# Named PSUM bank pairs, the sine table at the first cosine, a third block transposed whole, and one rounding of each softmax batch on VectorE

## The chip, the core and the metric

The kernel runs on one core of a Trainium2 chip. Its metric is the device time of one execution in microseconds. Engines: PE (TensorE), PEld (its weight loads), DVE (VectorE), ACT (ScalarE), POOL (GpSimd), SP (SyncE, which issues all DMAs here). PSUM has eight banks; a tile of 128x1024 f32 takes two.

## The reference

Two stages, all float32. The first is a causal convolution over 7 rows whose weights are a softmax over 7 numbers given for each row and head; the second is a feed-forward network whose activation is `h * cos(h)`.

```python
# x (8,4096,192), weight_gen (8,4096,8,7): 8 heads of 24 columns, 7 taps
w = np.exp(weight_gen - max);  w = w / (sum(w) + 1e-9)
out = np.einsum('bshk,bskhg->bshg', w, x_unf)      # x_unf: the row and the 6 before it
x2 = out.reshape(32768, 192)
h = x2 @ w_in            # (192, 2048)
g = h * np.cos(h)
return g @ w_out         # (2048, 192)
```

## The kernel before, in words

The 32768 rows are 64 blocks of 512 rows (4 rows on each of 128 partitions). A block's 2048 hidden columns are 8 pairs of 128-column chunks. The main loop runs over all 512 pairs; one turn of it, `i`, is called a period here (block `i // 8`, pair `i % 8`). The order of the instructions on each engine is the order in which the code emits them; nothing is moved later.

In period `i` these things are emitted, in this order:

- ACT rounds `h` of pair i-1 plus 0.25 to an integer (`act_turns`, L365), and writes the rounded-to-fp32r copy of `h * cos` of pair i-2 (`act_hi`, L383). In one period of every 32 (step `EXP`) ACT also takes the exponential of the next softmax batch here (L205).
- DVE subtracts the integer from `h` (`dve_fraction`, L369); ACT takes the sine of that fraction (`act_cos`, L373); DVE writes the remainder of pair i-2 in bf16 (`dve_lo`, L387), the last reader of that `h`; DVE multiplies `h` by the cosine, in place in PSUM (`dve_g`, L376).
- In periods 1 to 8, pieces of the two weight matrices are converted as well (`two_parts`): an Abs on ACT into PSUM (L130), a shift (L132) and two bit operations (L136, L140) on DVE, casts on ACT (L143, L145) and a subtraction on POOL (L146) one period later. The PSUM scratch of the three DVE steps is a tile of the same pool as `h`, taken in `make_room`.
- PE multiplies: the first half of the products of `h` of pair i (`ffn_in_first`, L338), the sums over the hidden columns for pair i-6's quarter (`ffn_out`, L417), and the second half of `h` (`ffn_in_second`, L355). SP holds an empty instruction behind the first half, which the second half waits for (`traded`). ACT copies finished sums out of PSUM every second period (`evacuate`, L440 and L444); the next sums need the bank.
- POOL does two or three steps of the convolution of a later block (`attention`, L257 products and L272 additions, 13 instructions a block).

The pool `ps_h` has three pairs of banks under one name; a tile gets the pair that became free first when its first instruction comes up. In a period without conversions, `h` of pair i takes the pair of banks that pair i-3 left. `ps_m` holds the sums in the other two banks.

A block's convolution result is transposed by PE before it can be multiplied. Blocks 1 and 2 (`WHOLE = 2`) are transposed by eight 128x128 transposes in one go (`transpose_all`, L308) in pair 5 of the block before, into the banks that `h` takes next, and are copied out by ACT (L664); their remainder is made on DVE (L299). From block 3 on, the transposes are small 64x64 pieces (L317) between the sums of block b-2, sixteen for a block, and the remainder is made on POOL (L299). POOL's convolution of block 3 has to be emitted by period 14 for that.

Ahead of the loop a prologue converts the first pieces, does the convolution of block 0 (three rows on DVE, one on POOL) and takes the first exponentials. ACT keeps one set of function tables; a load (ACT_TABLE_LOAD) stands where the next function is in another set.

Of the kernel before, what the change touches and what calls it, by code (L numbers as in the profile page):

```python
# [20 lines left out]
P = 128  # L21
# [22 lines left out]
def tile_softmax_conv_then_cos_ffn(  # L44
# [25 lines left out]
    HALF = NPAIR // 2  # L70
    LAG = 6
    TR = 5
    WHOLE = 2
    TMP = 4
    CW = 512

# [2 lines left out]
    work = ctx.enter_context(tc.tile_pool(name="work", bufs=2))  # L79
    ps_h = ctx.enter_context(tc.tile_pool(name="ps_h", bufs=3, space=bass.MemoryType.PSUM))  # L80
    ps_m = ctx.enter_context(tc.tile_pool(name="ps_m", bufs=1, space=bass.MemoryType.PSUM))


    x_v = x.rearrange("n (q r) d -> q n (r d)", r=RPP)
# [27 lines left out]

    room = []

    def make_room():
        sizes = ps_h.tile([P, 2, CT], F32, name="h")
        bits = work.tile([P, 2, CW], F32, name="t1", tag="turn", bufs=TMP)
        room[:] = [(sizes[:, n, 0:CW].bitcast(I32), bits[:, n, :].bitcast(I32)) for n in range(2)]

# [179 lines left out]
        eng.tensor_tensor(  # L299
            out=lo[:, :, cs], in0=t, in1=hi[:, :, cs].bitcast(F32), op=ALU.subtract)  # L300

    def transpose_all(b, tr=None):
        xa = mixed[b]
        if tr is None:
            tr = ps_h.tile([P, 2, CT], F32, name="h")
        for part in range(2):
            for r in range(R):
                nc.tensor.transpose(tr[:, part, r * P:(r + 1) * P], xa[:, r, columns(part)], ident)  # L308
        transposed.add(b)
        return tr  # L310
# [18 lines left out]
    def ffn_in_first(i, h=None):  # L329

        b, pair = divmod(i, NPAIR)
        x_hi, x_lo = xT[b]
        if h is None:
            h = ps_h.tile([P, 2, CT], F32, name="h")
        for m, (w, v) in enumerate(((wa_hi, x_lo), (wa_lo, x_hi), (wa_hi, x_hi))):
            for q in range(2):
                rs = slice(q * D2, (q + 1) * D2)
                nc.tensor.matmul(  # L338
                    h[:, q, :], lhsT=w[rs, chunk(pair, q)], rhs=v[rs, q, :],
                    start=(m == 0), stop=False, skip_group_check=True)  # L340
        hs[i] = h
        traded(h)
# [19 lines left out]
    def act_turns(i):  # L362
        t = work.tile([P, 2, CT], F32, name="turn", bufs=TMP)
        turns[i] = t
        nc.scalar.activation(out=t.bitcast(I32), in_=hs[i], func=AF.Identity, bias=0.25, scale=1.0)  # L365

    def dve_fraction(i):
        t = turns[i]
# [101 lines left out]
    def last_half():  # L470

        b = NB - 1
        tiles = [ps_h.tile([P, 2, CT], F32, name="h") for _ in range(2)]
        for p in range(HALF):
            for lo in range(2):
                g = g_parts[b * NPAIR + HALF + p][lo]
                for t in range(R):
                    acc = tiles[t // 2][:, t % 2, 0:(D if lo else 2 * D)]
                    for n in range(2):
                        fc = 2 * (HALF + p) + n  # L480
                        nc.tensor.matmul(
                            acc, lhsT=g[:, n, t * P:(t + 1) * P], rhs=(wo_b if lo else wo)[:, fc, :],
                            start=(p == 0 and lo == 0 and n == 0),
                            stop=(p == HALF - 1 and lo == 1 and n == 1), skip_group_check=True)
        fin = work.tile([P, R, D], F32, name="fin")
        for t in range(R):
            old = sums.pop((b, t // 2))[:, t % 2] if t % 2 else sums[(b, t // 2)][:, 0]
            part_ = work.tile([P, 2, CT], F32, name="part1", bufs=2)
            part = part_[:, 0, 0:2 * D]
            nc.vector.tensor_tensor(out=part, in0=tiles[t // 2][:, t % 2, 0:2 * D], in1=old, op=ALU.add)  # L490
            (nc.vector if t == R - 1 else nc.gpsimd).tensor_tensor(
                out=fin[:, t, :], in0=part[:, 0:D], in1=part[:, D:2 * D], op=ALU.add)
            if t % 2:
                nc.sync.dma_start(out=o_v[:, :, (b * R + t - 1) * D:(b * R + t + 1) * D],
                                  in_=fin[:, t - 1:t + 1, :].rearrange("p r d -> p (r d)"))
# [19 lines left out]
    def all_of(*steps):  # L515
        steps = list(steps)
        while steps:
            steps = [s for s in steps if next(s, steps) is not steps]
# [11 lines left out]
    def load_weights(period):  # L530
        for when, at, load, args in late:
            if when == period:
                converts.setdefault(at, []).append(load(*args))
# [1 line left out]
    nc.scalar.activation(out=early, in_=early, func=AF.Exp)  # L535

    RV = 3
    own = ps_h.tile([P, 2, CT], F32, name="h")
    own = own.rearrange("p a b -> p (a b)")
    own_acc = own[:, 0:RV * D].rearrange("p (r d) -> p r d", d=D)  # L540
    own_taps = own[:, R * D:R * D + RV * H * K].rearrange("p (n k) -> p n k", k=K)
# [13 lines left out]
    def go_on(steps, n):  # L555
        for _ in range(n):
            next(steps, None)
# [11 lines left out]
    all_of(sm1)  # L569
    bg = attentions()  # L570
    go_on(bg, 1)
    make_room()
    go_on(w_a0, 1)
    go_on(w_b0, 1)
    all_of(mix_v)
    tr = transpose_all(0)
    go_on(w_a0, 3)
    go_on(w_b0, 3)
    first = split(0, tr, slice(0, CT), nc.vector)
# [1 line left out]
    all_of(w_a0, w_b0)  # L581
    all_of(first)
    go_on(sm2, 2)
    make_room()
    go_on(w_a1, 4)
    go_on(sm2, 1)
    nc.scalar.activation(out=early, in_=early, func=AF.Sin)
    all_of(w_a1)
    go_on(bg, 4)

    N = NB * NPAIR
# [4 lines left out]
    for i in range(N + LAG + 1):  # L596
# [11 lines left out]
        converts_now = converts.get(i, ())  # L608
        h_now = None
        if converts_now:  # L610
            h_now = ps_h.tile([P, 2, CT], F32, name="h")

        whole = None
        if pair == TR and b + 1 <= WHOLE:
            until_mixed(b + 1)
            whole = transpose_all(b + 1, h_now)
        if 0 <= j and j % (2 * R) == 0 and WHOLE < j // (2 * R) + 2 < NB:
            until_mixed(j // (2 * R) + 2)

        def products():  # L620
            if b < NB and pair == 0:
                assert b in transposed
            if whole is not None and j >= 0:

                ffn_out(j)
                ffn_in_first(i, whole)
            elif j >= N - HALF:
                if j == N - HALF:
                    last_half()
                return  # L630
            elif busy and EXP + 2 <= step <= EXP + 3:

                ffn_out(j, rest=False)
                ffn_in_first(i)
                ffn_out(j, rest=True)
            else:
                if i < N:
                    ffn_in_first(i, h_now if whole is None else whole)
                if j >= 0:
                    ffn_out(j)  # L640
            if i < N:
                ffn_in_second(i)
            if j in stores:
                stores.pop(j)()
            if j >= 0:
                evacuate(j)


        early_sums = busy and step == EXP + 1
        if 0 <= i - 1 < N:  # L650
            act_turns(i - 1)
        if early_sums:
            products()
# [15 lines left out]
        if 0 <= i - 2 < N:  # L669
            dve_lo(i - 2)  # L670
        if converts_now:
            make_room()
        for c in converts_now:
            next(c)
        all_of(*converts.pop(i - 1, ()))
        for c in now:
            next(c)
        splits.extend(later)
        if 0 <= i - 1 < N:
            dve_g(i - 1)  # L680
        for _ in range(3):
            for c in converts_now:
# [3 lines left out]
            break  # L686
        if not early_sums:
            products()
        load_weights(i)
        if step in SOFTMAX and step != EXP or NPAIR - 2 <= i < NPAIR + 1:  # L690
            next(sm, None)
        for _ in range(3 if i < 12 or i < 64 and i % 4 == 0 else 2):
            next(bg, None)


# [39 lines left out]
```

## Time and profile before

| | |
|---|---|
| median of 3 runs | 2276.68 us (2276.4 to 2276.85) |
| profiled execution | 2278.1 us, span 2276.3 us |
| busy | PE 2212.3 (97%), PEld 2017.7, DVE 1904.1 (84%), ACT 1896.8 (83%), POOL 2003.6 (88%) |
| granted TensorE clock | 0.992 of full speed over the span |

The page cuts the span into 40 slices of 57 us. PE is at 3 and 7 tenths in the first two and at 9 or more in all others:

```profile
PE   3799999999999999999999999999999999999998
DVE  7788888888888888888888888888888888888887
ACT  4688888888888888888888888888888888888886
POOL 7799989998999989989899899989989899899941
PEclk9799999999999999999999999999999999999999
```

A digit is the busy share in tenths, and in the line PEclk the granted clock in tenths of full speed.

### The profile page before, as it was taken

Reading aid. Unit: us, or ns where it says so; the run is one execution under the profiler, and the core shown is the slowest. Engines: PE = TensorE matmul, PEld = TensorE weight load, DVE = VectorE, ACT = ScalarE, POOL = GpSimd, SP = SyncE. Lnnn points to the kernel's source line nnn. Section 1 sums busy time; section 2 is a strip of 40 time slices with the busy share of each in tenths; the row PEclk is TensorE's granted clock in tenths of the full one; section 3 lists DMA queues with packets and bytes.
Section 4 is the critical chain, followed back from the end, with each engine's and each line's share of the span. In section 5 each row is a group of like instructions: output and inputs, shape, how many; then the busy total and the mean of one; then the engine's idle time right before and its main releaser. Section 6 shows DMA issues by size and latency. Waiting matters only on the chain.

```text
span 2276.3 us, 60636 instructions
## 1 busy us (share of the span) xinstructions
PE 2212.3 (97%) x26504; PEld 2017.7 (89%) x26504; DVE 1904.1 (84%) x1647; ACT 1896.8 (83%) x2129; POOL 2003.6 (88%) x1464
## 2 busy tenths in 40 slices
PE   3799999999999999999999999999999999999998
PEld 2688888889898898998999999998998989999887
DVE  7788888888888888888888888888888888888887
ACT  4688888888888888888888888888888888888886
POOL 7799989998999989989899899989989899899941
PEclk9799999999999999999999999999999999999999
DMA  6211221211211211211211212212212212212100
GB/s 155 56 44 41 50 51 33 58 43 33 58 41 43 50 40 44 50 47 37 58 30 46 58 28 56 50 28 57 50 34 50 58 26 50 58 26 52 33 9 22
DMA packets 25767, 105.55 MB, mean 46 GB/s; under 512 B 2734, under 2 KB 6566, under 8 KB 25502
## 3 DMA queue, kind: packets, MB, share of 16 engines
q1 hardware_dynamic: 25502, 101.67, 18.2%
q8 instruction: 208, 3.41, 0.6%
q14 instruction: 57, 0.47, 0.1%
HBM read 76.50 MB, written 25.17 MB: 45 GB/s over the span
## 4 chain that ended last, share of the span: by engine, by line
PE 68%; POOL 19%; ACT 7%; issue 3%; DVE 3%; DMA 0%; POOLq 0%; SPq 0%; ACTq 0%; DVEq 0%
PE acc L417 32%; PE h L355 23%; PE h L338 12%; POOL xa L272 6%; POOL pr L257 5%; POOL part L456 2%; ACT turn L365 2%; ACT part L440 2%; POOL x_lo L299 1%; ACT ghi L383 1%; POOL fin L457 1%; DVE turn L369 1%; ACT turn L373 1%; POOL taps L202 1%; DVE glo L387 1%
## 5 line engine op out<-in xcount | busy, mean ns | idle before, releaser
L369 DVE TENSOR_TENSOR turn<-h,turn 128x1024 f32<-128x1024 f32 x512 | 625.8, 1222 | 295.5 <-ACT turn L365 295.3
L417 PE MATMUL acc<-wo,ghi 64*128 64x384 f32 x8112 | 810.2, 336 | 4.3 <-ACT part L440 4.1
L417 PEld LDWEIGHTS acc<-wo,ghi 64*128 64x128 f32 x8112 | 738.2, 185 | 43.7 <-ACT part L440 13.5
L272 POOL TENSOR_TENSOR xa<-xa,pr 128x768 f32<-128x768 f32 (+1 forms) x384 | 704.2, 1834 | 0.7
L373 ACT ACTIVATE turn<-turn 128x1024 f32<-128x1024 f32 x512 | 543.8, 1062 | 182.4 <-DVE turn L369 179.0
L376 DVE SCALAR_TENSOR_TENSOR h<-h,turn 128x1024 f32<-128x1024 f32 x512 | 631.0, 1232 | 49.2 <-ACT turn L373 49.2
L365 ACT ACTIVATE turn<-h 128x1024 int32<-128x1024 f32 x512 | 525.6, 1027 | 141.7 <-PE h L355 130.2
L387 DVE TENSOR_TENSOR glo<-h,ghi 128x1024 bf16<-128x1024 f32 x512 | 622.4, 1216 | 9.9 <-ACT ghi L383 9.9
L257 POOL TENSOR_TENSOR pr<-xt,taps 128x768 f32<-128x768 f32 (+1 forms) x384 | 587.1, 1530 | 11.9
L383 ACT CAST ghi<-h 128x1024 fp32r<-128x1024 f32 x512 | 518.2, 1012 | 15.5 <-DVE h L376 15.5
L417 PE MATMUL acc<-wo_b,glo 64*128 64x192 bf16 x8112 | 432.4, 243 | 0.0
L456 POOL TENSOR_TENSOR part<-part,part 128x768 f32<-128x768 f32 x126 | 233.3, 1851 | 165.0 <-ACT part L440 138.8
L417 PEld LDWEIGHTS <-glo 64*128 64x128 bf16 x8112 | 334.9, 94 | 22.2 <-issue 10.7
L355 PE MATMUL h<-x_lo,wa_hi 64*128 64x512 f32 x1024 | 254.4, 480 | 0.6
L338 PE MATMUL h<-x_lo,wa_hi 64*128 64x512 f32 x1024 | 217.7, 408 | 30.9 <-DVE glo L387 25.1
L440 ACT COPY part<-acc 128x1024 f32<-128x1024 f32 x244 | 243.1, 996 | 0.0
L355 PE MATMUL h<-x_lo,wb_hi 64*128 64x512 f32 x1024 | 212.3, 397 | 0.0
L338 PE MATMUL h<-x_hi,wa_lo 64*128 64x512 f32 x1024 | 210.8, 393 | 1.5 <-POOL wa_lo L146 1.5
L355 PE MATMUL h<-x_hi,wa_hi 64*128 64x512 f32 x1024 | 211.8, 396 | 0.0
L338 PE MATMUL h<-x_hi,wa_hi 64*128 64x512 f32 x1024 | 211.3, 394 | 0.0
L355 PE MATMUL h<-x_hi,wa_lo 64*128 64x512 f32 x1024 | 209.3, 392 | 0.0
L355 PE MATMUL h<-x_hi,wb_lo 64*128 64x512 f32 x1024 | 209.1, 391 | 0.0
(74 smaller groups left out, 2149.4 us busy)
## 6 DMA issues: line engine op xcount, KB each, us to landing
xt<-in_x_dram SPq DMA_DIRECT2D x62, 960.0 KB, 6.8
out_dram<-fin SPq DMA_DIRECT2D x63, 384.0 KB, 3.4
taps<-in_weight_gen_dram SPq DMA_DIRECT2D x15, 448.0 KB, 4.9
raw<-in_moe_w_out_dram SPq DMA_DIRECT2D x8, 384.0 KB, 4.5
raw<-in_moe_w_in_dram SPq DMA_DIRECT2D x10, 256.0 KB, 10.4
xt<-in_x_dram SPq DMA_DIRECT2D x1, 768.0 KB, 10.1
xt<-in_x_dram SPq DMA_DIRECT2D x1, 540.0 KB, 5.7
raw<-in_moe_w_in_dram SPq DMA_DIRECT2D x4, 128.0 KB, 4.8
```

The costliest lines, as they stand in the source:

```text
L257: eng.tensor_tensor(out=dst.rearrange("p r (h g) -> p r h g", h=H), in0=xt[:, k + ra:k + rb, :].rearrange("p r (h g) -> p r h g", h=H), in ...
L272: eng.tensor_tensor(out=acc if k < K else xa, in0=acc, in1=old[:, ra:rb], op=ALU.add)
L338: nc.tensor.matmul(h[:, q, :], lhsT=w[rs, chunk(pair, q)], rhs=v[rs, q, :], start=(m == 0), stop=False, skip_group_check=True)
L355: nc.tensor.matmul(h[:, 1 - q, :], lhsT=w[rs, cs], rhs=v[rs, q ^ middle, :], start=False, stop=(m == len(prods) - 1), skip_group_check=True)
L365: nc.scalar.activation(out=t.bitcast(I32), in_=hs[i], func=AF.Identity, bias=0.25, scale=1.0)
L369: nc.vector.tensor_tensor(out=t, in0=hs[i], in1=t.bitcast(I32), op=ALU.subtract)
L373: nc.scalar.activation(out=t, in_=t, func=AF.Sin, bias=SIN_BIAS, scale=SIN_SCALE)
L376: nc.vector.scalar_tensor_tensor(out=hs[i], in0=hs[i], scalar=TWO_PI, in1=turns.pop(i), op0=ALU.mult, op1=ALU.mult)
L383: nc.scalar.copy(out=hi, in_=hs[i])
L387: nc.vector.tensor_tensor(out=lo, in0=hs.pop(i), in1=hi.bitcast(F32), op=ALU.subtract)
L417: nc.tensor.matmul(to, lhsT=g[rs, n, t * P:(t + 1) * P], rhs=w[rs, fc, :], start=(lo == 0 and c == 0 and (whole or s == 0)), stop=(lo == 1 ...
L440: nc.scalar.copy(out=part, in_=acc)
```

## The change

Five edits. The PSUM pairs get names: `h` of pair i always takes pair `i % 3`, and the scratch of a conversion in period i takes that of pair i-2, whose last reader stands just ahead of it in DVE's order. The load of the sine table is no longer asked for in the prologue, and the last conversion of the prologue is finished ahead of the exponential of the third softmax instead of behind it. Block 3 joins the blocks transposed whole. The number of POOL's convolution steps in periods 0 to 19 is set anew. And in the period of a softmax batch's exponential, the rounding of that period's own `h` is done by DVE, behind the products, and `dve_g` of the pair before stands behind it; ACT leaves this rounding out in the period after.

```diff
-    WHOLE = 2
+    WHOLE = 3
+    def h_banks(k):
+        return ps_h.tile([P, 2, CT], F32, name="h", tag=f"h{k % 3}", bufs=1)
-    def make_room():
-        sizes = ps_h.tile([P, 2, CT], F32, name="h")
+    def make_room(k):
+        sizes = h_banks(k)
...
-            h = ps_h.tile([P, 2, CT], F32, name="h")
+            h = h_banks(i)
...
+    def dve_turns(i):
+        t = work.tile([P, 2, CT], F32, name="turn", bufs=TMP)
+        turns[i] = t
+        nc.vector.tensor_scalar(out=t.bitcast(I32), in0=hs[i], scalar1=0.25, scalar2=None, op0=ALU.add)
...
     go_on(sm2, 2)
-    make_room()
-    go_on(w_a1, 4)
+    make_room(1)
+    all_of(w_a1)
     go_on(sm2, 1)
-    nc.scalar.activation(out=early, in_=early, func=AF.Sin)
-    all_of(w_a1)
     go_on(bg, 4)
...
-        if 0 <= i - 1 < N:
+        if 0 <= i - 1 < N and i - 1 not in turns:
             act_turns(i - 1)
...
         if converts_now:
-            make_room()
+            make_room(i - 2)
...
-        if 0 <= i - 1 < N:
+        if 0 <= i - 1 < N and not exps:
             dve_g(i - 1)
...
         if not early_sums:
             products()
+        if exps:
+            dve_turns(i)
+            dve_g(i - 1)
...
-        for _ in range(3 if i < 12 or i < 64 and i % 4 == 0 else 2):
+        for _ in range(3 if 5 <= i < 20 or i < 64 and i % 4 == 0 else 2):
             next(bg, None)
```

## Rows read from the trace of the kernel before

**Rows 1.** PE's waits over the whole span: line, releaser, total us, times, longest.
```profile
PE h L338 <- DVE glo L387: 25.1, 21, 3.7
```

**Rows 2.** Timeline, period 2 (start, us, engine, line, what, [idle before]).
```profile
37.50 1.23 DVE L369 TENSOR_TENSOR turn<-h,turn 128x1024 f32<-128x1024 f32 x1
38.64 1.22 DVE L387 TENSOR_TENSOR glo<-h,ghi 128x1024 bf16<-128x1024 f32 x1
40.00 0.79 PE L338 MATMUL h<-x_lo,wa_hi 64*128 64x512 f32 x2 [3.72 <-DVE glo L387]
40.98 1.29 DVE L132 TENSOR_SCALAR h<-h 128x512 int32<-128x512 int32 x2
43.71 1.15 DVE L140 SCALAR_TENSOR_TENSOR t<-raw,h 128x512 int32<-128x512 int32 x2
44.03 0.63 PE L355 MATMUL h<-x_hi,wb_hi 64*128 64x512 f32 x2
```

**Rows 3.** Line L132, a conversion's first step (ns min/median/max: 256, 384, 512 columns).
```profile
L132 DVE TENSOR_SCALAR h<-h x15: 422/567/699, 20.1 to 95.7; 128x384 int32<-128x384 int32 x8, 128x512 int32<-128x512 int32 x5, 128x256 int32<-128x256 int32 x2
```

**Rows 4.** Timeline, end of the prologue and period 1: PE and ACT.
```profile
28.63 1.28 ACT L587 ACT_TABLE_LOAD   x1
28.99 0.63 PE L355 MATMUL h<-x_hi,wb_hi 64*128 64x512 f32 x2
30.54 1.01 ACT L365 ACTIVATE turn<-h 128x1024 int32<-128x1024 f32 x1
32.91 1.06 ACT L373 ACTIVATE turn<-turn 128x1024 f32<-128x1024 f32 x1 [1.36 <-DVE turn L369]
```

**Rows 5.** Timeline of POOL, period 2.
```profile
48.52 1.27 POOL L146 TENSOR_TENSOR wa_lo<-t,wa_hi 128x512 fp32r<-128x512 f32 x1
```

**Rows 6.** Timeline, periods 5, 6 and 9.
```profile
64.23 1.03 ACT L664 COPY part<-h 128x1024 f32<-128x1024 f32 x1
73.12 0.79 PE L338 MATMUL h<-x_lo,wa_hi 64*128 64x512 f32 x2 [3.64 <-DVE glo L387]
79.94 0.42 PE L355 MATMUL h<-x_hi,wb_hi 64*128 64x512 f32 x2
100.58 0.41 PE L338 MATMUL h<-x_lo,wa_hi 64*128 64x512 f32 x2
```

**Rows 7.** A stretch of 10 us: PE, PEld, DVE, ACT, POOL busy (instructions), clock, DMA.
```profile
80.00:90.00 10.00, 6.27 (x48) 5.40 (x46) 6.02 (x7) 4.62 (x7) 5.05 (x4) 0.66 0.01 2
```

**Rows 8.** Timeline, transposes: block 2 whole, blocks 3 and 4 in pieces, POOL's last additions.
```profile
118.01 1.09 PE L308 MATMUL h<-ident,xa 128*128 128x128 f32 x8
126.14 0.28 PE L317 MATMUL acc<-ident,xa 64*128 64x64 f32 x2 [0.17 <-POOL xa L272]
149.44 3.79 POOL L272 TENSOR_TENSOR xa<-xa,pr 128x768 f32<-128x768 f32 x2
160.24 0.22 PE L317 MATMUL acc<-ident,xa 64*128 64x64 f32 x2
```

**Rows 9.** Timeline of one softmax batch, PE, DVE and ACT.
```profile
607.55 0.40 PE L355 MATMUL h<-x_hi,wb_hi 64*128 64x512 f32 x2
609.94 0.82 PE L417 MATMUL acc<-wo_b,glo 64*128 64x192 bf16 x16
610.34 1.23 DVE L376 SCALAR_TENSOR_TENSOR h<-h,turn 128x1024 f32<-128x1024 f32 x1 [3.19 <-ACT turn L373]
611.42 1.00 ACT L440 COPY part<-acc 128x1024 f32<-128x1024 f32 x1
612.48 1.68 PE L417 MATMUL acc<-wo,ghi 64*128 64x384 f32 x16 [0.29 <-ACT part L440]
613.38 1.23 DVE L387 TENSOR_TENSOR glo<-h,ghi 128x1024 bf16<-128x1024 f32 x1 [0.60 <-ACT ghi L383]
614.75 0.50 PE L338 MATMUL h<-x_lo,wa_hi 64*128 64x512 f32 x2 [0.21 <-DVE glo L387]
620.31 1.23 DVE L387 TENSOR_TENSOR glo<-h,ghi 128x1024 bf16<-128x1024 f32 x1
```

More of the change, by code (lines that the diff above doesn't have):

```diff
@@ L300, in split, with transpose_all @@
             out=lo[:, :, cs], in0=t, in1=hi[:, :, cs].bitcast(F32), op=ALU.subtract)
-    def transpose_all(b, tr=None):
+    def transpose_all(b, k, tr=None):
         xa = mixed[b]
         if tr is None:
-            tr = ps_h.tile([P, 2, CT], F32, name="h")
+            tr = h_banks(k)
         for part in range(2):
@@ L472, in last_half @@
         b = NB - 1
-        tiles = [ps_h.tile([P, 2, CT], F32, name="h") for _ in range(2)]
+        tiles = [h_banks(N + n) for n in range(2)]
         for p in range(HALF):
@@ L537, in tile_softmax_conv_then_cos_ffn @@
     RV = 3
-    own = ps_h.tile([P, 2, CT], F32, name="h")
+    own = h_banks(2)
     own = own.rearrange("p a b -> p (a b)")
@@ L575, in tile_softmax_conv_then_cos_ffn @@
     all_of(mix_v)
-    tr = transpose_all(0)
+    tr = transpose_all(0, 2)
     go_on(w_a0, 3)
@@ L583, in tile_softmax_conv_then_cos_ffn @@
     go_on(sm2, 2)
-    make_room()
-    go_on(w_a1, 4)
+    make_room(1)
+    all_of(w_a1)
     go_on(sm2, 1)
-    nc.scalar.activation(out=early, in_=early, func=AF.Sin)
-    all_of(w_a1)
     go_on(bg, 4)
@@ L610, in tile_softmax_conv_then_cos_ffn @@
         if converts_now:
-            h_now = ps_h.tile([P, 2, CT], F32, name="h")
+            h_now = h_banks(i)
         whole = None
@@ L615, in tile_softmax_conv_then_cos_ffn @@
             until_mixed(b + 1)
-            whole = transpose_all(b + 1, h_now)
+            whole = transpose_all(b + 1, i, h_now)
         if 0 <= j and j % (2 * R) == 0 and WHOLE < j // (2 * R) + 2 < NB:
@@ L671, in tile_softmax_conv_then_cos_ffn @@
         if converts_now:
-            make_room()
+            make_room(i - 2)
         for c in converts_now:
```

## The prediction, made before the changed kernel was run

> **What bounds the kernel now.** PE is busy for 97% of the span, so the first question is where its other 64 us are. The view of waits (PE alone) names one cause ahead of all others: the first half of `h` waits for `dve_lo`, 25.1 us in 21 waits [rows 1]. The timeline then shows two kinds. Six of them are in the conversion periods 2, 3, 4, 6, 7 and 8, with 3.6 to 3.7 us each [rows 2, 6], some 22 us; the other 15, one in each softmax batch, are 0.2 us each [rows 9]. The rest of the span PE runs through, at 4.26 us a period (eight periods lie between the transposes at 126.14 and 160.24 [rows 8]), and no edit touches what a period costs there. So the change can act in two places: the first 105 us and the batches.
>
> Why the head waits: in period 2 the conversion's scratch gets the pair of banks that the scratch of period 1 left, and `h(2)` has to take that of `h(0)`, whose last reader is `dve_lo` at 38.64 in the same period; PE starts at 40.00 [rows 2]. But `dve_lo` stands behind the fraction of `h(1)`, and this needs all of `h(1)`. So PE and DVE take turns.
>
> **The change part by part**
>
> *Named pairs, the head (with the table and POOL's steps).* `h(i)` now takes the pair that the scratch of period i-1 left. It starts when the last bit operation (L140) of period i-1 is over, and PE works beside the DVE of period i. DVE's own chain becomes the bound. From one fraction to the first conversion step are 3.48 us (37.50 to 40.98 [rows 2]); a conversion of 256, 384 or 512 columns takes three steps of 0.42, 0.57 or 0.70 [rows 3], so 1.3, 1.7 or 2.1 us (the row of period 2 checks: 40.98 to 44.86 for 512 and 384 columns together, 3.88 against 3.8). Periods 1 to 8 convert 2.1, 3.8, 3.8, 3.4, 3.0, 1.7, 1.7, 1.7.
>
> The start: without the table load in ACT's queue, the rounding of `h(0)` waits only for PE (28.99 + 0.63 = 29.62) instead of 30.54 [rows 4], so the chain begins 0.9 earlier and the first fraction starts at 30.8. The load itself falls between that rounding and the first cosine, where ACT sits idle for 1.36 us and the load takes 1.28 [rows 4]: nothing. Bounds: 1.3 lost if it hid nowhere, 0.9 won as taken.
>
> Then, fraction to end of L140: period 1 30.8 + 3.48 + 2.1 = 36.4; period 2 43.7; period 3 51.0. In period 3 PE is held by the remainder of the weights on POOL (48.52 [rows 5]); it comes 3.6 earlier (2.1 because the cast ahead of it in the prologue no longer stands behind the load and the exponential, 1.5 because period 1 issues one product less), ends at 46.1, and `h(3)` at 50.4, so the next fraction starts at 51.5. Period 4 58.4. Period 5 has ACT's copy of the whole transposes (1.03 [rows 6]) ahead of the cosine, which costs DVE 0.8: 65.7. Period 6: `h(6)` and the first sums take what they took, 73.12 to 80.36, 7.24 [rows 6], so it ends at 73.0, its fraction starts at 74.1, L140 of period 7 ends at 79.3. One reciprocal of the softmax, 0.9; L140 of period 8 at 85.4. `h(9)` starts at 85.5 instead of 100.58 [rows 6], **15.0 us earlier**; from there no scratch is taken and PE is the bound again. Bounds: nothing left of the 22 us of waits but the 0.9, were DVE and ACT to hold PE as long; 17 if POOL and ACT never do.
>
> Behind conversions, SP's order matters too: a weight load waits for DVE's last read of its buffer, and the empty instruction of the next period's `h` stands behind it. That read is L140, which `h` now waits for anyway; so this costs nothing.
>
> *Block 3 transposed whole.* PE gets eight transposes in period 21, 1.09 us [rows 8], and in period 13, which did the same, the products came some 0.4 later still by their changed order: +1.5. Sixteen small transposes go, about 0.04 a period over eight periods, -0.3, and with them the waits for POOL at 126.14 (0.17 in the row, 0.5 with the weight load's) [rows 8], -0.5. Sum **+0.7**, bounds -0.5 and +2. ACT's copy and DVE's remainder (some 1 us each) lie beside sums in a period without a softmax. What it buys is cover: with the head 15 us shorter, PE would want block 3 at 111, while POOL, even without the 12 us that it waited for the conversions, has it at about 114 to 117. Now it is wanted in period 21, near 141. Block 4 is the next: POOL ended its additions at 153.2 and PE read them at 160.24 [rows 8]; 12 us earlier for POOL and 14 for PE leaves 5 of the 7 us of margin. Were it gone, PE would lose what POOL is late, up to 5 us.
>
> *DVE's rounding in each batch (15 batches).* In the period of the exponential, ACT has two table loads and an exponential ahead of the cosine, and DVE waits 3.19 us for it, until 610.34 [rows 9]. `h` of that period is complete at 607.55 + 0.40 = 607.95 [rows 9]. The trace has no DVE instruction that turns f32 into int32. Its price lies between 1.0 (ACT's for the same tile [rows 4]) and 1.4 (two shifts of 512 columns from PSUM [rows 3]); I take 1.23, DVE's for a tile of that size that it narrows to bf16 [rows 2, 9]. It ends at 609.2, 1.1 ahead of the cosine; so `dve_g`, the only thing queued behind its wait that others need, is not later. Below that no gain: DVE's idle time is the price. What goes is on ACT: the copy of the sums, 611.42, stood behind this rounding, and the sums were over at 609.94 + 0.82 = 610.76 [rows 9]. It starts at 610.8, and 0.6 earlier come `act_hi`, `dve_lo` (613.38, whose 0.60 of idle time goes with it [rows 9]) and PE's products, which start 1.37 behind it (614.75 [rows 9]). PE's waits of 0.29 and 0.21 are those in front. From 613.38 to 620.31 DVE runs without a gap (six instructions of 1.16 [rows 9]), and this last one frees the banks of the products four periods after the exponential, so DVE keeps 0.57 of the gain and not more. 15 x 0.57 = **-8.6**; bounds 0 and -9.8 (0.65 each).
>
> **Sum.** -15.0 + 0.7 - 8.6 = -22.9. The profiled execution took 2278.1, with 1.8 around its span, so it would take 2255.2; the runs' median is 1.4 below it, and so the forecast is **2254**.
>
> A place where the Trainium skill speaks against this: ScalarE: Activation LUTs, section What ACT_TABLE_LOAD costs, gives a switch of tables 2.66 us, a load of 1.28 and a drain. By that the moved load would stick out of its idle time by an estimated 1.3 us, and the result would be 2255. The trace has the rounding at 30.54 start 1.91 behind the load, with two instructions between [rows 4], so no such drain stands there.
>
> **The rivals**
>
> *PE stays at 1.2 GHz.* From 80 to 90 us the granted clock was 0.66 of full speed, with PE busy for 6.27 of 10 [rows 7]. If it stays at the lower level through periods 6 to 8, each takes twice 4.26: 65.7, 74.2, 82.7, and `h(9)` starts at 91.3, 5.8 later: **2260**. For it: periods 2 to 5 leave PE idle for a third of the time. Against it: in period 6 the waits were 3.64 [rows 6], and now none is over 2.5. The Trainium skill (TensorE: Matmul & The Clock Gate, What's actually happening) says that the half rate is the resting state and that activity lifts it; the stretch of rows 7 agrees with it. Chance 0.13.
>
> *The batches give nothing.* The copy of the sums or `act_hi` waits for something else, or DVE's own run sets the pace anyway. Then **2262**. For it: DVE is full behind the batch for seven instructions. Against it: it starts that run with an idle gap of just the amount that goes. 0.11.
>
> *The pairs free little.* The scratch pair is free, but the head is held elsewhere (POOL's remainders, the `turn` buffers which rounding and scratch share, POOL late for block 4), and two thirds of the 15 us are lost: **2264**. For it: POOL was busy nearly throughout from 30 to 80. 0.09.
>
> *Slower.* The rounding on DVE is far longer than rows of its size. It stands ahead of `dve_g`, and everything of the batch behind that. From an end at 610.34 on, 2.4 us long, each further microsecond costs every batch one. With the head at -14.3, the kernel is slower once a batch loses over 0.95, that is from 3.9 us on; at 5.0 it is 15 x 2.0 = 31 - 14: **2293**. For it: no row has this conversion. Against it: narrowing to bf16 costs DVE nothing over f32 [rows 2]. 0.04.
>
> **How the numbers follow.** The forecast has 0.61, with 2250 to 2258 for itself; the four rivals hold 0.37, and 0.02 are for gains that cancel. The range goes down to 2246 (head -17, block 3 -0.5, batches -9.8, and 3 for what I mis-sized) and up to 2265, which takes in three rivals. A difference under 0.2% (4.6 us) counts as none, as a measurement can't tell it. Faster 0.93, same 0.03, slower 0.04.
>
> **What would show it.** PE's waits for `dve_lo` in the head gone, and waits of 2 to 3 us for L140 in periods 2 to 5 in their place; `h(9)` near 85.5; the table load right ahead of the first cosine; no wait of PE for a convolution result; in each batch an int32 write of DVE inside the gap of 3.2 us, `dve_g` not later against the exponential, the copy of the sums right behind the sums, and 32 periods 0.6 shorter. I am wrong if the head's clock stays low, if POOL stops PE near period 22, or if `dve_g` waits for the new rounding.

## The result, and the profile after

The changed kernel takes **2257.72 us** (median of 5 runs, 2256.61 to 2258.11), the kernel before in the same job 2276.85 (2276.4 to 2277.25): ratio 0.9915, 95% interval 0.9901 to 0.9928. That is 19.1 us less, where 22.9 were forecast; the time lies inside the range and inside the forecast's own (2250 to 2258), near its upper end. The profiled execution took 2257.9 with a span of 2256.1, 20.2 shorter than before.

The busy times of the changed kernel, from its page:

```profile
PE 2203.8 (98%) x26496; PEld 2009.9 (89%) x26496; DVE 1922.0 (85%) x1663; ACT 1886.0 (84%) x2111; POOL 2001.4 (89%) x1460
```

PE's waits after, the view of [rows 1] (total us, times, longest). The line numbers have moved: up to L365 of before, a line stands 4 lower now (L338 is L342, L355 is L359, L140 is L144, L299 is L303), from L369 to L456 it stands 10 lower (L387 is L397, L417 is L427), and L664 is L672.

```profile
PE h L342 <- DVE t L144: 14.1, 6, 3.8
PE h L312 <- DVE t L144: 3.0, 1, 3.0
PE h L342 <- DVE glo L397: 1.7, 10, 0.3
PE h L342 <- POOL wa_lo L150: 1.3, 1, 1.3
```

The wait for `dve_lo` fell from 25.1 to 1.7, and 17.1 us of waits for the conversion's last step (L144) came in its place. That such waits would come was forecast; their sizes were not all right. Expected were 2 to 3 us in each of periods 2 to 5. It was 3.66, 3.63, 0.96 and 3.02 there, some 1.0 each in periods 6 and 7, and 3.76 in period 8. No wait for a convolution result stands in the view behind the prologue.

So PE waits only a little less than before. From the first half of `h(1)` to that of `h(9)` the kernel before takes 69.90 us and the changed one 57.84. Of these 12.1 us, 6.0 are waits; the other 6.1 are PE's own time for the same products, the second number of each row (PE, PEld, DVE, ACT, POOL busy, clock, DMA share, GB/s; first before, then after). Which part of the 6.1 lay on the path, the rows do not tell.

```profile
30.68:100.58 69.90, 43.92 (x248) 31.41 (x250) 51.28 (x63) 38.78 (x56) 58.76 (x40) 0.76 0.26 71
```
```profile
29.24:87.08 57.84, 37.83 (x250) 26.32 (x248) 51.00 (x63) 40.48 (x58) 53.56 (x37) 0.73 0.34 90
```

The head of the changed kernel, timeline (start, us, engine, line, what, [idle before]):

```profile
30.53 1.28 ACT L383 ACT_TABLE_LOAD   x1
31.87 1.06 ACT L383 ACTIVATE turn<-turn 128x1024 f32<-128x1024 f32 x1
36.46 0.50 PE L342 MATMUL h<-x_lo,wa_hi 64*128 64x512 f32 x2 [3.66 <-DVE t L144]
58.26 1.22 DVE L379 TENSOR_TENSOR turn<-h,turn 128x1024 f32<-128x1024 f32 x1
58.49 1.94 PE L312 MATMUL h<-ident,xa 128*128 128x128 f32 x8 [3.02 <-DVE t L144]
62.46 1.23 DVE L386 SCALAR_TENSOR_TENSOR h<-h,turn 128x1024 f32<-128x1024 f32 x1 [1.86 <-ACT turn L383]
66.88 1.23 DVE L379 TENSOR_TENSOR turn<-h,turn 128x1024 f32<-128x1024 f32 x1 [0.27 <-ACT turn L369]
72.04 1.68 DVE L303 TENSOR_TENSOR x_lo<-part,x_hi 128x1024 fp32r<-128x1024 f32 x1
73.64 1.07 DVE L214 TENSOR_REDUCE den<-taps 128x128 f32<-128x896 f32 x1
74.74 0.46 DVE L217 TENSOR_SCALAR den<-den 128x128 f32<-128x128 f32 x1
75.12 1.21 DVE L379 TENSOR_TENSOR turn<-h,turn 128x1024 f32<-128x1024 f32 x1
80.48 0.79 PE L342 MATMUL h<-x_lo,wa_hi 64*128 64x512 f32 x2 [3.76 <-DVE t L144]
81.90 2.79 PE L427 MATMUL acc<-wo,ghi 64*128 64x384 f32 x16
```

The load stands right ahead of the first cosine and costs nothing there (the rounding ends at 30.5, and the cosine would have waited for the fraction until 31.8 anyway, as 30.61 + 1.23). The fraction of period 4 starts at 58.26 (forecast 58.4), that of period 6 at 75.12 (74.1), `h(9)` at 87.08 (85.5; before 100.58 [rows 6]). PE is at its lower clock level in much of this stretch; two places matter below. The transposes of block 1 take 1.94 (those of block 3 below take 1.09; granted clock 0.50 of full speed from 58.49 to 60.43), and the start of `h(8)` and the sums of period 8 take 0.79 and 2.79 for the usual 0.50 and 1.59 (0.50 from 80.48 to 85.50).

The transposes of block 3 (whole, now in period 21), POOL's last additions for blocks 3 and 4, and PE's first read of block 4, the answer to [rows 8]:

```profile
111.87 3.76 POOL L276 TENSOR_TENSOR xa<-xa,pr 128x768 f32<-128x768 f32 x2
137.71 3.75 POOL L276 TENSOR_TENSOR xa<-xa,pr 128x768 f32<-128x768 f32 x2
140.37 1.09 PE L312 MATMUL h<-ident,xa 128*128 128x128 f32 x8
148.16 0.22 PE L321 MATMUL acc<-ident,xa 64*128 64x64 f32 x2
```

Block 4 is done at 141.5 and read at 148.16: 6.7 us of margin, where 5 were forecast. One softmax batch after, the answer to [rows 9]:

```profile
594.42 1.23 DVE L375 TENSOR_SCALAR turn<-h 128x1024 int32<-128x1024 f32 x1 [0.83 <-PE h L359]
595.68 1.06 ACT L383 ACTIVATE turn<-turn 128x1024 f32<-128x1024 f32 x1
596.77 1.23 DVE L386 SCALAR_TENSOR_TENSOR h<-h,turn 128x1024 f32<-128x1024 f32 x1 [1.13 <-ACT turn L383]
597.24 1.02 ACT L450 COPY part<-acc 128x1024 f32<-128x1024 f32 x1 [0.20 <-PE acc L427]
599.20 1.22 DVE L397 TENSOR_TENSOR glo<-h,ghi 128x1024 bf16<-128x1024 f32 x1
```

The new rounding is in DVE's gap; 1.13 us of the gap are left in front of `dve_g`, which still waits for the cosine. The copy of the sums starts 0.20 behind them, and PE's wait of 0.21 is gone.

Where the gain is, from the start of the second half of `h` in each period (the first row of L355 or L359 of the period, in both timelines):

| start of period | before | after | gain | what happened since the row above |
|---|---|---|---|---|
| 1 | 33.35 | 31.14 | 2.2 | start |
| 9 | 103.29 | 89.82 | 13.5 | conversions |
| 14 | 126.85 | 113.02 | 13.8 | before waited for POOL's block 3 |
| 16 | 135.42 | 121.94 | 13.5 | DVE's remainder of block 2 in period 14 (below) |
| 20 | 152.40 | 138.76 | 13.6 | small transposes gone |
| 21 | 156.65 | 144.55 | 12.1 | whole transposes of block 3 |
| 31 | 199.09 | 187.17 | 11.9 | its remainder |

So the head gave 13.5, and block 3 and its neighbours took 1.6 of it back. The batches can be read at the load of the exponential's table (first the changed kernel, then the one before; first and last start):

```profile
L209 ACT ACT_TABLE_LOAD  x15: 1283/1283/1283, 182.3 to 2094.2; - x15
```
```profile
L205 ACT ACT_TABLE_LOAD  x15: 1283/1283/1283, 194.2 to 2114.4; - x15
```

The gain grows from 11.9 to 20.2 over 14 batches, 0.59 each; the fifteenth gives nothing more (the span ends 20.2 shorter). 11.9 + 8.3 = 20.2. The profiled execution of before was 1.3 above its median here, that of after 0.2, hence 19.1 between the medians.

### The profile page after: what moved, and what is told of

It reads as the page before. It is cut to its first block, busy times and chain, and to the rows that moved or that the text cites. A ratio compares the mean times of both kernels' runs of the same rounds, so it can differ in the third digit from the quotient of the medians.

```text
span 2256.1 us, 60616 instructions
## 1 busy us (share of the span) xinstructions
PE 2203.8 (98%) x26496; PEld 2009.9 (89%) x26496; DVE 1922.0 (85%) x1663; ACT 1886.0 (84%) x2111; POOL 2001.4 (89%) x1460
## 4 chain that ended last, share of the span: by engine, by line
PE 94%; DVE 2%; ACT 2%; POOL 1%; issue 1%; DMA 0%; SPq 0%; POOLq 0%; DVEq 0%; ACTq 0%
PE acc L427 45%; PE h L359 31%; PE h L342 16%; PE acc L321 1%; DVE glo L397 1%; ACT part L450 1%; ACT ghi L393 1%; POOL xa L276 1%; POOL pr L261 1%; PE h L491 0%; DVE turn L379 0%; DMA xt<-in_x_dram 0%; DVE h L140 0%; DVE h L136 0%; PE h L312 0%
## 5 line engine op out<-in xcount | busy, mean ns | idle before, releaser
L427 PE MATMUL acc<-wo,ghi 64*128 64x384 f32 x8112 | 807.2, 335 | 0.3 <-ACT part L454 0.3
L427 PEld LDWEIGHTS acc<-wo,ghi 64*128 64x128 f32 x8112 | 736.7, 185 | 35.9 <-ACT part L450 3.1
L386 DVE SCALAR_TENSOR_TENSOR h<-h,turn 128x1024 f32<-128x1024 f32 x512 | 631.0, 1233 | 20.3 <-ACT turn L383 20.3
L397 DVE TENSOR_TENSOR glo<-h,ghi 128x1024 bf16<-128x1024 f32 x512 | 622.5, 1216 | 2.7 <-ACT ghi L393 1.7
L369 ACT ACTIVATE turn<-h 128x1024 int32<-128x1024 f32 x497 | 510.2, 1027 | 125.5 <-PE h L359 118.6
L261 POOL TENSOR_TENSOR pr<-xt,taps 128x768 f32<-128x768 f32 (+1 forms) x384 | 589.5, 1536 | 11.9
L393 ACT CAST ghi<-h 128x1024 fp32r<-128x1024 f32 x512 | 518.0, 1012 | 14.2 <-DVE h L386 14.2
L427 PE MATMUL acc<-wo_b,glo 64*128 64x192 bf16 x8112 | 431.1, 243 | 0.0
L427 PEld LDWEIGHTS <-glo 64*128 64x128 bf16 x8112 | 333.5, 94 | 23.0 <-issue 11.0
L359 PE MATMUL h<-x_lo,wa_hi 64*128 64x512 f32 x1024 | 253.0, 477 | 0.7
L342 PE MATMUL h<-x_lo,wa_hi 64*128 64x512 f32 x1024 | 217.3, 407 | 20.5 <-DVE t L144 14.1
L359 PE MATMUL h<-x_lo,wb_hi 64*128 64x512 f32 x1024 | 211.8, 397 | 0.0
L342 PE MATMUL h<-x_hi,wa_lo 64*128 64x512 f32 x1024 | 210.1, 392 | 1.3 <-POOL wa_lo L150 1.3
L359 PE MATMUL h<-x_hi,wa_hi 64*128 64x512 f32 x1024 | 211.1, 395 | 0.0
L342 PE MATMUL h<-x_hi,wa_hi 64*128 64x512 f32 x1024 | 210.5, 393 | 0.0
L359 PE MATMUL h<-x_hi,wb_hi 64*128 64x512 f32 x1024 | 208.6, 390 | 0.0
L359 PE MATMUL h<-x_hi,wb_lo 64*128 64x512 f32 x1024 | 208.5, 390 | 0.0
## 6 DMA issues: line engine op xcount, KB each, us to landing
xt<-in_x_dram SPq DMA_DIRECT2D x1, 768.0 KB, 10.5
```

The costliest lines, as they stand in the source:

```text
L261: eng.tensor_tensor(out=dst.rearrange("p r (h g) -> p r h g", h=H), in0=xt[:, k + ra:k + rb, :].rearrange("p r (h g) -> p r h g", h=H), in ...
L342: nc.tensor.matmul(h[:, q, :], lhsT=w[rs, chunk(pair, q)], rhs=v[rs, q, :], start=(m == 0), stop=False, skip_group_check=True)
L359: nc.tensor.matmul(h[:, 1 - q, :], lhsT=w[rs, cs], rhs=v[rs, q ^ middle, :], start=False, stop=(m == len(prods) - 1), skip_group_check=True)
L386: nc.vector.scalar_tensor_tensor(out=hs[i], in0=hs[i], scalar=TWO_PI, in1=turns.pop(i), op0=ALU.mult, op1=ALU.mult)
L393: nc.scalar.copy(out=hi, in_=hs[i])
L397: nc.vector.tensor_tensor(out=lo, in0=hs.pop(i), in1=hi.bitcast(F32), op=ALU.subtract)
```

## The experiments

Every run was timed in five rounds beside the kernel before (2276.65 to 2277.26 in the four jobs). The intervals of the ratios are about 0.0013 to either side, 3 us; smaller differences between kernels are read from the starts of periods in the traces. "Gain" is that of the table above. A trace is one execution, and the head differs between executions of the same instructions: `a1`, `a5`, `a3` and `a6` below have the head of the changed kernel, and their gain at period 9 is 13.5, 14.1, 14.7 and 14.9 against its 13.5; `b1` has the head of the kernel before, and its gain there is 2.2. So a difference of up to 2 us in the head is not told by one trace alone.

**One part undone or done alone: the batches.** `a1_act_rounding` is the changed kernel without DVE's rounding:

```diff
-        if 0 <= i - 1 < N and not exps:
+        if 0 <= i - 1 < N:
             dve_g(i - 1)
-        if exps:
-            dve_turns(i)
-            dve_g(i - 1)
```

> The changed kernel with the rounding of each softmax batch back on ACT and dve_g back in its old place. Theory (the rounding takes the copy of the sums out of ACT's way, 0.6 us a batch): 32 periods take 137.16 again instead of 136.56, 15 batches give back 8.9, so 2266.6; the head is as in the changed kernel, h(9) at 87.1. Rival (the batches got shorter through the named pairs, which fix the order in which banks come free): 2257.7, unchanged.

Measured: 2265.75, ratio 0.995 (0.9938 to 0.9963). `b1_dve_rounding` is the kernel before with `dve_turns` and this, and nothing else of the change:

```diff
-        if 0 <= i - 1 < N:
+        if 0 <= i - 1 < N and i - 1 not in turns:
             act_turns(i - 1)
-        if 0 <= i - 1 < N:
+        if 0 <= i - 1 < N and not exps:
             dve_g(i - 1)
+        if exps:
+            dve_turns(i)
+            dve_g(i - 1)
```

> The kernel before with the rounding on DVE alone added. Theory: 15 x 0.59 = 8.9 off, 2267.9, and h(9) stays at 100.6. Rival (the two edits need each other): 2276.8.

Measured: 2268.59, 0.9963 (0.995 to 0.9975). 8.0 lost without it, 8.6 gained by it alone, forecast 8.6. In `a1` the table loads run from 182.3 to 2102.4, as far apart as before; in `b1` from 192.0 to 2103.6, as close as in the changed kernel. This part depends on no other.

**The named pairs.** `a2_one_pool` gives all tiles one name again:

```diff
-        return ps_h.tile([P, 2, CT], F32, name="h", tag=f"h{k % 3}", bufs=1)
+        return ps_h.tile([P, 2, CT], F32, name="h")
```

> The changed kernel with the three pairs of banks under one name again, all other edits kept. Theory (the scratch holds h two periods back): PE's waits of 3.6 us for dve_lo are back in periods 2, 3, 4, 6, 7, 8; only the 1 to 2 us of the prologue stay won, h(9) at 98.5 to 99.5, so 2269 to 2270. Rival (the head got faster by the table and by POOL's steps): h(9) near 88, 2258 to 2260.

Measured: 2266.91, 0.9957 (0.9944 to 0.9969). The gain at period 9 falls from 13.5 to 5.0, and the old wait is back (PE's waits). I had expected 1 to 2 us to stay and a time of 2269 to 2270; so the other edits are worth more in the head than I thought, and the pairs, undone, 8.5 of its 13.5.

```profile
PE h L342 <- DVE glo L397: 26.0, 15, 6.1
```

`b2_named_pairs` is the kernel before with the named pairs alone (`h_banks` as in the change, and all calls that go with it):

```diff
-            h = ps_h.tile([P, 2, CT], F32, name="h")
+            h = h_banks(i)
-            make_room()
+            make_room(i - 2)
```

> The kernel before with the named pairs alone. Theory: the head is DVE's chain, 0.9 later for the table, and POOL's remainders come one product later, so h(9) at 88 to 90, 11 to 12 us earlier; then POOL has block 3 at 115 to 118 while PE wants it at 126.1 - 11.5 = 114.6 in period 14, a wait of 1 to 4; 2276.8 - 11.5 + 2.5 = 2268. Rival (POOL is never late, so WHOLE = 3 buys nothing): no wait in period 14, 2265.

Measured: 2269.70, 0.9968 (0.9955 to 0.998). The gain at period 9 is 9.5, and 9.1 behind period 14, where PE waited for POOL for 0.6 us; I had expected more of that wait. The head, too, is less than expected: `h(9)` starts at 90.99, where 88 to 90 was forecast and the changed kernel has 87.08. Of these 3.9 us, 1.3 are there when `h(3)` starts (45.21 against 43.89), as the prologue is the old one, and 2.6 come in period 3: PE's waits for a weight's remainder on POOL rose to 4.4 (1.3 in the changed kernel).

```profile
PE h L342 <- POOL wa_lo L150: 4.4, 2, 3.9
```

**Block 3.** `a3_whole2` takes this edit back:

```diff
-    WHOLE = 3
+    WHOLE = 2
```

> The changed kernel with blocks 1 and 2 alone transposed whole, block 3 in pieces again. Theory: POOL ends block 3 at 115.6, PE reads it in period 14 at 126.1 - 13.4 = 112.7, a wait of 2.9; the whole transposes of block 3 (1.5 in period 21, 0.2 behind it) go: 2257.7 + 2.9 + 0.3 - 1.7 = 2259. Rival (the cover was not needed, as in the run with the pairs alone, which waited 0.6): 2256.5, faster than the changed kernel.

Measured: 2260.88, 0.9928 (0.9916 to 0.9941). PE wants block 3 in period 14 and waits for POOL:

```profile
PE acc L321 <- POOL xa L276: 3.4, 1, 3.4
```

The gain falls from 14.85 to 10.5 over periods 14 and 15, by 4.3, where the edit costs the changed kernel 1.5. So the cover that the prediction saw in it is real and worth more than its price.

**The table and the last conversion.** `a4_sine_early` puts both back:

```diff
-    all_of(w_a1)
+    go_on(w_a1, 4)
     go_on(sm2, 1)
+    nc.scalar.activation(out=early, in_=early, func=AF.Sin)
+    all_of(w_a1)
     go_on(bg, 4)
```

> The changed kernel with the sine table loaded in the prologue again, ahead of the last cast. Theory: ACT's queue holds the first rounding and the cast 0.9 to 2.1 longer, POOL's remainder in period 3 comes 2 later, and h(9) 1 to 2 later: 2258.7 to 2259.7. Rival A (DVE's chain takes it up before period 9): 2257.7. Rival B (a table switch costs 2.7, as the Trainium skill has it in ScalarE: Activation LUTs, What ACT_TABLE_LOAD costs): 2260.4.

Measured: 2259.61, 0.9924 (0.9911 to 0.9936); gain at period 9 12.1, so 1.4 less than the changed kernel's and less than that of all five executions of its head. The second half of `h(1)` starts at 33.04 for 31.14. The time can't tell the theory from rival B, which is 0.8 away; but in the changed kernel the cosine starts 1.34 behind the start of the load (30.53 and 31.87 above), so no second 1.3 us stand there.

**How long DVE's rounding may be.** `a5_round_twice` and `a6_round_thrice` write the same rounding two and three times:

```diff
-        nc.vector.tensor_scalar(out=t.bitcast(I32), in0=hs[i], scalar1=0.25, scalar2=None, op0=ALU.add)
+        for _ in range(2):                                                  # a6: range(3)
+            nc.vector.tensor_scalar(out=t.bitcast(I32), in0=hs[i], scalar1=0.25, scalar2=None, op0=ALU.add)
```

> The changed kernel with DVE's rounding of each batch done twice into the same tile. Theory (it lies in the gap that DVE waits for the cosine, 1.13 us of it left): the second ends at about the same time as the cosine, 0 to 0.1 a batch, 2257.7 to 2259.2. Rival (DVE's time in the batch is not free, as it runs full behind it): 15 x 1.2 = 18 more, 2276.

> The same with three roundings. Theory: from an end behind the cosine on each microsecond costs every batch one: 3 x 1.2 = 3.6 against a gap of 2.35 is 1.2 a batch, 18 in all, 2276. Rival (the following periods take it up, since DVE has 0.65 us to spare in each): under 0.4 a batch, 2257.7 to 2264.

(In `a5` and `a6` the lines behind L375 stand one lower: L376 is the rounding, L384 the cosine, L387 `dve_g`.)

Measured: 2257.84, 0.9917 (0.9903 to 0.993) and 2275.11, 0.9994 (0.9985 to 1.0003). The batch's rounding in the one and the other (DVE; the time is that of the group):

```profile
593.80 2.48 DVE L376 TENSOR_SCALAR turn<-h 128x1024 int32<-128x1024 f32 x2 [0.83 <-PE h L359]
```
```profile
596.59 3.75 DVE L376 TENSOR_SCALAR turn<-h 128x1024 int32<-128x1024 f32 x3 [0.83 <-PE h L359]
```

Behind the doubled rounding `dve_g` starts at 596.20, without a wait, and it costs nothing; a third one costs 17.3 us, 1.15 in each of 15 batches. That is the slower rival's mechanism with the threshold it gave: free to 2.4 us, level with the kernel before near 3.9 us (here 3.75, and 2275.1 against 2276.7). Its condition was false: one rounding takes 1.23.

**POOL's steps.** `a8_old_steps` restores the old numbers of convolution steps.

```diff
-        for _ in range(3 if 5 <= i < 20 or i < 64 and i % 4 == 0 else 2):
+        for _ in range(3 if i < 12 or i < 64 and i % 4 == 0 else 2):
```

> The changed kernel with POOL's convolution steps as they were before (three a period in periods 0 to 11, then two). Theory of the prediction: one more product ahead of the weight's remainder in period 2 brings it 1.5 us later, PE's first half of h(3) with it, and the head is up to 1 us longer: 2258.2 to 2259. Rival: PE in period 3 waits for DVE's bit operations and not for POOL, as its waits in the changed kernel say (3.63 us for DVE, 1.3 for POOL in all), so there is no difference: 2257.7.

Measured: 2261.43, 0.9929 (0.9917 to 0.9942), more than either theory; four of its five executions took 2261.3 to 2261.6, one 2259.0. The step that I named is there: POOL's remainder starts at 46.55 and no longer at 44.70, and period 3 is 1.85 late. Then it grows: `h(9)` starts at 90.63, 3.55 late. Read along DVE's chain, 1.75 of this stand at `dve_g` of period 5 (64.21 against 62.46). Another 0.45 come with `h(5)`, which PE works at its lower level to the end (the next fraction starts at 69.08 against 66.88). The largest step, 1.14, is DVE's remainder of block 1, which takes 2.82 here and 1.68 in the changed kernel. With the old numbers of steps one of POOL's additions starts just ahead of it (POOL and DVE, period 6 of `a8`):

```profile
74.12 1.84 POOL L276 TENSOR_TENSOR xa<-xa,pr 128x768 f32<-128x768 f32 x1
74.22 2.82 DVE L303 TENSOR_TENSOR x_lo<-part,x_hi 128x1024 fp32r<-128x1024 f32 x1
76.04 2.41 POOL L261 TENSOR_TENSOR pr<-xt,taps 128x768 f32<-128x768 f32 x1
```

DVE's instruction ends at 77.04, 1.08 behind POOL's addition, and the undisturbed one of `a6` below takes 1.22 in all. `h(8)` is then 3.3 late, and PE waits 4.89 for it:

```profile
83.82 0.79 PE L342 MATMUL h<-x_lo,wa_hi 64*128 64x512 f32 x2 [4.89 <-DVE t L144]
```

The last 0.2 come in period 8. So a delay of under 2 us in the head was nearly doubled, by 1.1 us through DVE and POOL getting in each other's way and by some 0.65 through PE's clock.

**The work on DVE in period 6.** `a7_split_pool` makes the remainder of whole blocks on POOL, `a9_split_den_pool` moves the sums of the third softmax there as well, and `a10_first_pool` moves the remainder of block 1 alone:

```diff
-            later.append(split(b + 1, t, slice(0, CT), nc.vector))
+            later.append(split(b + 1, t, slice(0, CT), nc.gpsimd))                          # a7, a9
-    sm2 = softmax(3 * R, 3 * R + RW, nc.gpsimd)
+    sm2 = softmax(3 * R, 3 * R + RW, nc.gpsimd, early=False)                                # a9
-            later.append(split(b + 1, t, slice(0, CT), nc.vector))
+            later.append(split(b + 1, t, slice(0, CT), nc.vector if b else nc.gpsimd))      # a10
```

> The changed kernel with the remainder of the blocks transposed whole made on POOL instead of DVE. Theory (DVE's chain bounds the head, and this remainder of 1.68 us is the part of it that the prediction had too small): the fraction of h(6) comes 1.0 to 1.7 us earlier, PE's wait in front of period 8 (3.76) becomes shorter and its sums run less at 1.2 GHz, and the 0.4 and 0.15 us that periods 16 and 24 lose beside such a remainder go too. h(9) near 85.0, in all 2255 us (2254 to 2256.5). Rival (POOL is what the head and block 4 wait for next): POOL's own steps come 2 to 3 us later for each block, PE waits for a convolution result or a weight's remainder, and the time is 2258 to 2260.

> The run with POOL's remainder, and also the sums of the third softmax on POOL, which takes another 1.5 us out of DVE's periods 6 and 7. If DVE bounds the head there, h(9) comes 1 us earlier still and the time is 2254 (2253 to 2255.5). If POOL is the bound by now, 2258 or more, with PE waiting for a convolution result.

> The changed kernel with only the remainder of block 1 (period 6) made on POOL; those of blocks 2 and 3 stay on DVE. The run with all three on POOL had h(9) 0.7 us earlier than the changed kernel and then lost 8.2 us in period 16, where POOL reached the remainder of block 2 too late. Theory (two separate effects): the first stays and the second goes, so h(9) starts near 86.4, period 16 takes 4.7 us, and the time is 2257.0 (2255.5 to 2258), at best just under the changed kernel. Rival (POOL's 2.4 us in period 6 are what made it late in period 16 as well): PE waits for POOL in period 16 again or in block 4, and the time is 2259 to 2264.

Measured: 2264.62, 0.9946 (0.9932 to 0.9959); 2267.78, 0.9958 (0.9946 to 0.9971); 2258.41, 0.9919 (0.9906 to 0.9933). My theory for these was wrong: none is better than the changed kernel. `a7` loses its time in period 16 (its gain falls from 14.2 to 5.6), where PE waits 6.2 us for block 2's remainder on POOL. `a9` loses 6.6 us of its gain earlier, between periods 9 and 11, where POOL comes late to a piece of the second weight matrix, and 3.6 more in period 16 (PE):

```profile
96.46 1.01 PE L427 MATMUL acc<-wo,ghi 64*128 64x384 f32 x4 [4.13 <-POOL wo L150]
```

And in `a10`, where neither happens, DVE got next to nothing for the instruction of 1.68 that it gave away: from one fraction to the next it takes 8.04 (67.18 to 75.22) for 8.24 (66.88 to 75.12) in the changed kernel, because a small instruction takes the time (POOL and DVE, period 6):

```profile
72.82 2.40 POOL L303 TENSOR_TENSOR x_lo<-part,x_hi 128x1024 fp32r<-128x1024 f32 x1
73.44 1.85 DVE L217 TENSOR_SCALAR den<-den 128x128 f32<-128x128 f32 x1
```

L217 takes 0.46 in the changed kernel; here it ends with POOL's instruction (75.29 and 75.22). Nor was the 0.7 us that `a10` was to keep from `a7` a gain of DVE: in `a7` DVE has done its conversion of period 8 at 86.26, in the changed kernel at 86.28, and `h(9)` came earlier (86.34) by PE's clock in period 8. `a9` has neither on DVE, and its fraction still starts only at 74.89: here DVE waits 1.99 for ACT's rounding, as `h(6)` itself came late (clock 0.50 from 60 to 70 us). But its period 8 shows what the clock is worth: with a wait of 2.40 in front of `h(8)` and not 3.76, the sums run at full clock,

```profile
80.27 0.50 PE L342 MATMUL h<-x_lo,wa_hi 64*128 64x512 f32 x2 [2.40 <-DVE t L144]
81.04 1.59 PE L427 MATMUL acc<-wo,ghi 64*128 64x384 f32 x16
```

and the second half of `h(8)` starts at 83.07, 2.5 before the changed kernel's 85.61, although `h(8)` started only 0.2 earlier.

## Why the prediction was right, and where its sizes were off

**Batches, -8.6: measured -8.3 (8.0 and 8.6 with the part undone and alone).** The price of 1.23 taken for the rounding, from the rows of its size, is 1.23 to the hundredth. The chain forecast (copy, `act_hi`, `dve_lo`, PE) moved as written.

**Head, -15.0: measured -13.5.** The mechanism was right: PE's wait for `dve_lo` is gone, DVE's chain bounds the periods, and up to the fraction of period 4 every time was within 0.2. Then `h(9)` comes 1.6 late. Two sizes were wrong, both for PE at the lower of its two levels (1.2 GHz) where I had it at full clock; and the path through period 6 was wrong, with the right length.

The first size is period 5: ACT's copy of the transposes "costs DVE 0.8". It cost 1.86, the wait in front of `dve_g` at 62.46, since the transposes took 1.94 for 1.09, and the copy and the cosine stand behind them. The conversion of period 5 is done at 66.62 for 65.7, and the next fraction starts at 66.88, another 0.27 behind, as it waits for the rounding of `h(5)`. From there to the conversion of period 8 DVE runs without a gap, so this 1.1 is in every later time, or nearly: period 6's fraction at 75.12 for 74.1, the conversion of period 7 done at 80.3 (79.78 + 0.55) for 79.3.

The path is that of period 6, and that it took the length I gave it is chance. I had taken PE's 7.24 from before; in fact DVE sets it, with its remainder of block 1 and the softmax's sums, 1.68 + 1.07 + 0.46, between two fractions. The sum had these at nothing, and of the 1.68, 0.46 are time beside POOL (below).

The second size is period 8: "now none is over 2.5", on which full clock rested there. PE waits 3.76 in front of `h(8)`, and the sums run at the lower level. DVE has done its conversion of period 8 at 86.28, 0.9 late. Elsewhere PE started 0.14 and 0.15 behind such a conversion (36.32 to 36.46, 80.33 to 80.48); `h(9)` starts, without a wait, only when PE is through at 87.08, so this is another 0.65.

`a6` has the same instructions up to the first batch, and its `h(9)` starts at 85.60, 1.48 earlier. Its transposes and its `dve_g` of period 5, and its remainder of block 1:

```profile
58.37 1.31 PE L312 MATMUL h<-ident,xa 128*128 128x128 f32 x8 [2.93 <-DVE t L144]
61.72 1.23 DVE L387 SCALAR_TENSOR_TENSOR h<-h,turn 128x1024 f32<-128x1024 f32 x1 [1.23 <-ACT turn L384]
71.75 1.22 DVE L303 TENSOR_TENSOR x_lo<-part,x_hi 128x1024 fp32r<-128x1024 f32 x1
```

`dve_g` is 0.74 earlier than in the changed kernel, but most of this is gone at the next fraction (66.60, 0.28 earlier), since `h(5)` runs at the lower level to its end. The remainder of block 1 then takes 1.22 and not 1.68: it starts 0.09 ahead of POOL's next product, while in the changed kernel it starts in the middle of one of POOL's (POOL 71.63 to 72.62, DVE from 72.04). So `h(8)` is 0.74 earlier, at 79.74. Period 8, the view of [rows 7] (PE, PEld, DVE, ACT, POOL busy, clock, DMA share, GB/s), first the changed kernel, then `a6`:

```profile
80.00:88.00 8.00, 7.52 (x60) 6.72 (x62) 6.22 (x8) 4.40 (x7) 7.92 (x6) 0.65 0.00 0
```
```profile
80.00:88.00 8.00, 8.00 (x78) 6.88 (x79) 6.59 (x8) 5.01 (x7) 7.92 (x6) 0.82 0.00 0
```

Here the other 0.74 are won. Of the 1.48, 1.02 are PE's clock and 0.46 DVE's remainder beside POOL. Over the five executions of this head the gain at period 9 lies between 13.5 and 14.9; the rival "PE stays at 1.2 GHz" was right in two places, not in three whole periods. What decides between such executions is not settled here.

**Block 3, +0.7: measured +1.5.** Its transposes cost what was said (period 21 takes 5.79 for 4.25, 1.54 more), and PE's waits for POOL gave back 0.4 (forecast 0.5), the small transposes about 0.2 (0.3). What was missing are 0.4 in period 16 and 0.15 in period 24, one period or two behind a remainder on DVE that I had put "beside sums" for nothing. `dve_lo` follows it closely, and PE waits for that (0.26 in front of `h(16)`).

Sum: -13.5 + 1.5 - 8.3 = -20.3 (20.2 in the spans), 2.7 short of -22.9, made of 1.5, 0.8 and 0.3; the other 1.1 of the miss is by how much more the profiled execution of before stood above its median than that of after.

**Not summed, but shown.** Undone singly, the parts cost 9.2 (pairs), 8.0 (rounding), 3.7 (POOL's steps), 3.2 (block 3) and 1.9 (table and order): 26 in all for a change worth 19. In the head they nearly add: at period 9 the pairs alone gain 9.5 (`b2`) and all the rest without them 5.0 (`a2`), against 13.5 together. Block 3 is different: it costs 1.5 in the sum, and undoing it costs as well, as PE then waits for POOL. That is some 3 us of the 7; the rest is no more than the intervals of five such differences.

**The rivals.** "The batches give nothing" and "the pairs free little" fell to `b1` and `b2`. The slower one had the right threshold (`a6`) and a false condition.

## What to carry to other kernels

Where PE and another engine take turns because a buffer comes free too late, freeing the buffer leaves waits of another kind (17 of 25 us here): follow the other engine's whole queue, and price the PE instructions right behind each wait at both clock levels, above all those that the other engine itself waits for. Give an instruction to an engine that waits anyway, and test how much room it has by issuing it twice. Before moving work to a neighbour engine that is 88% busy, count what it delivers next and when that is wanted. And before changing when POOL does what, look at which of its instructions will stand beside those of DVE that read two tiles of SBUF: in `a8` that cost 1.1 us.

## What the runs showed of the hardware

**DVE and POOL block each other over SBUF.** In the changed kernel the remainder of block 2 on DVE meets POOL's additions and then POOL's next one:

```profile
115.10 1.62 DVE L303 TENSOR_TENSOR x_lo<-part,x_hi 128x1024 fp32r<-128x1024 f32 x1
115.59 2.82 POOL L466 TENSOR_TENSOR part<-part,part 128x768 f32<-128x768 f32 x1
```

POOL's additions end at 115.63, DVE's instruction 1.1 later (1.22 undisturbed, in `a6`), and POOL's next takes 2.82 for its usual 1.85. In `a10` the same two take 2.44 and 2.83, and PE waits 1.08 for `dve_lo` behind them; in `a8` the remainder of block 1 took 2.82. Whichever starts first goes through: in `a6` DVE's started 0.09 before POOL's product and took 1.22, and the product took 2.53 for its usual 1.54. This and L217 above, 0.46 made 1.85, look like one engine holding the other off for whole instructions. The Trainium skill (SBUF — State Buffer, section SBUF: two separate sides) says just this: a DVE instruction with two SBUF inputs, or in a mode that uses both ports, and one of POOL exclude each other for the whole instruction. The rows agree; the sum of the softmax (L214) ran beside POOL at 1.08 and was not held.

**The clock behind a wait is not told by its length.** In period 8 PE kept full clock behind a wait of 2.40 us (`a9`), fell within the sums behind 2.78 (`a7`: 2.31 and 1.53 for the two groups of sums), rose within them behind 3.28 (`a6`: 2.40 and 0.85), and stayed low through nearly all of them behind 3.76 (2.79 and 1.37). Yet `h(2)`, behind 3.66, took 0.50, the time at full clock, and in the kernel before two waits of the same length, in front of `h(7)` and `h(8)`, ended one at the lower level and one at full clock:

```profile
84.10 0.80 PE L338 MATMUL h<-x_lo,wa_hi 64*128 64x512 f32 x2 [3.73 <-DVE glo L387]
94.72 0.50 PE L338 MATMUL h<-x_lo,wa_hi 64*128 64x512 f32 x2 [3.73 <-DVE glo L387]
```

What it is worth: the same stretch, from `h(8)` to its second half, took 5.1 us in the changed kernel and 2.8 in `a9`.
